# A third buffer for squares, a seventh squared group, and a new written-out order in a fused attention and rational-activation kernel

## The chip, the cores and the metric

The kernel runs on one core of one Trainium2 chip. Every time is device time in microseconds (us) of one launch. Engines are named as in the profile: PE is TensorE's matmul, PEld its weight load, DVE is VectorE, ACT is ScalarE, POOL is GpSimd, SP issues loads and stores. Of the kernel before, three runs took 264.58, 264.75 and 264.84 us; the median is 264.75.

## The reference

```python
def phi(x):                                  # q, k: [4, 4, 1088, 32]; S1, S2: [8, 32]
    a = einsum('rd,bhsd->bhsr', S1, x)
    b = einsum('rd,bhsd->bhsr', S2, x)
    return einsum('bhsi,bhsj->bhsij', a, b).reshape(..., 64)
q_p, k_p = phi(q), phi(k)
kv  = einsum('bhsf,bhsd->bhfd', k_p, v);  z = sum(k_p, axis=2)
x   = einsum('bhsf,bhfd->bhsd', q_p, kv) / (einsum('bhsf,bhf->bhs', q_p, z) + 1e-6)
x   = x with its heads side by side          # [4352, 128]
h   = x @ w_in                               # [4352, 2048]
P   = a[0] + a[1]*h + a[2]*h**2 + a[3]*h**3
Q   = 1 + abs(b[0])*abs(h) + abs(b[1])*h**2
out = (P / (Q + 1e-6)) @ w_out               # [4352, 128], float32
```

## The kernel before, in words

**Tiling.** The 4352 tokens are cut into ten chunks: two of 256 tokens (labelled 0 and 0b), seven of 512 (1 to 7), and one of 256 that holds the 64 left-over tokens of each batch (8). A chunk goes through an attention stage and then through the activation in *groups*, numbered 0 to 22: one group is some of the 16 blocks of 128 hidden columns for the tokens of one chunk. Groups 0 to 3 are chunk 0 (512, 512, 1024 and 2048 elements per partition), group 4 is chunk 0b (4096), groups 5 to 18 are two for each of the chunks 1 to 7 (4096), groups 19 to 22 are chunk 8 (2048, 1024, 512, 512).

**Attention.** Keys of a batch (`k tr`, `k ev`, `k ab`, `k eva`, `k prod`, `kv`) give kv and z in PSUM, which `kvbd`, `zbd` (DVE), `zproj` (PE), `zspread` and `zrem` (DVE) turn into weights. Queries of a chunk go through `q tr` (PE), `q ev` (ACT copy to the tile qT, line 601), `q abc` (PE), `q eva` (ACT copy to the tile abc, line 618), four small DVE steps for the denominator (`q dpr`, `q dsum`, `q dinv`, `q scale`, lines 629 to 641), `q prod` (DVE, line 646), `qp tr`, `qp ev`, `x mm` and `x ev` (ACT copy to the tile xT, line 715).

**Activation of a group g.** `h` (PE, line 794) multiplies xT by w_in into PSUM, two at a time, and `hev` (ACT, line 800) copies that to the bf16 tile hb. After that u must become |b0||h| + |b1|h*h, then 1/Q through `ln` (ACT, line 833) and `exp` (ACT, line 837: exp of minus the logarithm), and y must become the numerator. The last product y*u (`n5`, DVE, line 829) goes to PE as `py` (line 857 or 852). There are four ways, chosen by a table TERMS:

- "2" (small groups): all on DVE.
- "2d" (groups 6, 8, 10, 12, 15, 17, 19): on DVE `abs` (bitwise, line 820), `lin` (line 825), `umul` (line 829), `n1` (line 841), `n2`, `n4`, `n5` (line 829). A constant is added to y by an accumulating DMA from the tile zeros (`dadd1`, POOL, line 897). The term a0/Q is not in y; it is a second set of matmuls on u with weights scaled by a0 (`pr`, 8 matmuls of 128x512).
- "t" (groups 5, 7, 11, 13, 16, 18): on DVE `abs` (bitwise), `sq` (h*h, line 914), `sqb` (h*h times |b1|/|b0|, line 919), `n1` and `n3` (the two linear forms a3*h*h+a1 and a2*h*h+a0, line 925), `n2` (times h, line 829), `n5`. Two accumulating DMAs from tiles named lin: `dq` adds sqb's result to u, `dy` adds n3's to y. `ln` takes |b0| as a scale from the tile b_rel. No `pr`.
- "s" (groups 4, 9, 14): as "t", but the absolute value is taken by ACT (`habs`, line 809, scale |b0|) instead of DVE, `sqb` multiplies by |b1|, and `ln` has the scale 1.

At the end of a chunk `oev` (ACT, line 862), `otr` (PE, line 867) and `otev` (ACT copy to the tile oT, line 872) turn the result, and SP stores it (line 1000). Chunk 8 comes out by token and needs only one ACT copy (`otev 8`, line 982) before its store.

**Buffers.** BUFS gives the number of buffers of each tile: lin 2, xT 3, qT 2, abc 2, oT 2 and others. A tile's next use waits until an earlier user of that buffer is done; for oT this is the store's DMA, for lin that was a DMA's source it is that DMA.

**Order.** All steps are collected in a plan, and a list ORDER of step numbers, written out by hand, says in which order they are issued. Each engine runs its own instructions strictly in that order. HOT gives numbers of dummy matmuls (line 1075) that stand between the last groups on PE.

Of the kernel before, what the change touches and what calls it, by code (L numbers as in the profile page):

```python
# [12 lines left out]
FP = mybir.dt.float32  # L13
# [110 lines left out]
def kernel(  # L124
# [13 lines left out]
    nc = tc.nc  # L138
# [19 lines left out]
    TERMS = {**{g:"2d" for g in range(4,20)}, **{g:"s" for g in (4,9,14)}, **{g:"t" for g in (5,7,11,13,16,18)}}  # L158
# [3 lines left out]
    HOT = [2, 6, 23, 4, 18, 4, 3]  # L162
# [20 lines left out]
    BUFS = dict(xT=3, hb=3, u=3, lin=2, y=3, L=1, h_ps=2, out_ps=1, w_ps=2, kv_ps=1,  # L183
                kq=3, v_aug=2, kT=2, ab=2, k_p=2, qT=2, abc=2, q_p=1, q_pT=2, den=2,
                o_sb=1, oT=2)
# [129 lines left out]
    b_rel = consts.tile([128, 3], FP, name="b_rel")  # L315
# [74 lines left out]
    def rel_b():  # L390
        nc.vector.tensor_scalar(out=b_rel[:, 0:1], in0=b_abs[:, 0:1], scalar1=1e-18, scalar2=None, op0=AX.max)
        nc.vector.reciprocal(out=b_rel[:, 1:2], in_=b_rel[:, 0:1])
        nc.vector.tensor_mul(out=b_rel[:, 2:3], in0=b_rel[:, 1:2], in1=b_abs[:, 1:2])

    c_b = plan.add("DVE", 100, abs_b, after=[ld["ab"]], rank=-5)
    c_b = plan.add("DVE", 300, rel_b, after=[c_b], rank=-5) if "t" in USED else c_b
# [187 lines left out]
    def add_queries(n, nt, srcs, weights, kv_lhs, load_steps, kv_steps, w_steps, rank, give=(), early=False,  # L584
# [58 lines left out]
        def product():  # L643
            abc = T["abc", n][:, :G, :]
            T["q_p", n] = tile_of(att, "q_p", [128, JC * H, R * R], FP)
            nc.vector.tensor_mul(out=T["q_p", n][:, :G, :].rearrange("p g (i j) -> p g i j", i=R),
                                 in0=abc[:, :, 0:R, None].broadcast_to([128, G, R, R]),
                                 in1=abc[:, :, None, R:2 * R].broadcast_to([128, G, R, R]))
# [69 lines left out]
        def rest(s):  # L718
            s = plan.add("DVE", 68 + 1067 * G // 16, product, after=[s, T.get(("prod", n - 1)) if pair == 1 else None], rank=rank + 0.02, take=["q_p"],
# [59 lines left out]
    def add_group(g, G):  # L779
# [27 lines left out]
        def s_abs():  # L807
            T["u", g] = tile_of(moe, "u", [128, GW], BF)
            nc.scalar.activation(out=T["u", g][:, :gw], in_=T["hb", g][:, :gw], func=ACT.Abs, scale=b_abs[:, 0:1])  # L809
# [21 lines left out]
        def ln(l0, lw):  # L831
            T["L", g, l0] = tile_of(moe, "L", [128, LW], FP)
            nc.scalar.activation(out=T["L", g, l0][:, :lw], in_=T["u", g][:, l0:l0 + lw], func=ACT.Ln, bias=one_ap,  # L833
                                 scale=b_rel[:, 0:1] if terms == "t" else 1.0)
# [81 lines left out]
        def s_scaled():  # L916
            T["even", g] = tile_of(moe, "lin", [128, GW], BF)
            by = b_rel[:, 2:3] if terms == "t" else b_abs[:, 1:2]
            nc.vector.tensor_scalar(out=even(), in0=sq(), scalar1=by, scalar2=None, op0=AX.mult)  # L919

        def s_affine(out, c1, c0):
            def f():
                if out is y:
                    T["y", g] = tile_of(moe, "y", [128, GW], BF)
                nc.vector.tensor_scalar(out=out(), in0=sq(), scalar1=a_sb[:, c1:c1 + 1], scalar2=a_sb[:, c0:c0 + 1],  # L925
                                        op0=AX.mult, op1=AX.add)
            return f

        if square:
            sp = plan.add("DVE", tt, s_first, after=[he], rank=g - 0.5, take=["lin"], name=f"sq {g}")  # L930
            d2 = plan.add("DVE", ts + 61, s_scaled, after=[sp, c_b], rank=g - 0.5, take=["lin"], name=f"sqb {g}")
            d = add_tile("dq", u, even, [ha, d2], g - 0.5, give=["lin"])
# [17 lines left out]
        if square:  # L950
            p = plan.add("DVE", ts + 121, s_affine(y, 3, 1), after=[sp, ld["ab"]], rank=g - 0.3, take=["y"], name=f"n1 {g}")
            t = plan.add("DVE", ts + 121, s_affine(sq, 2, 0), after=[sp, d2, p, ld["ab"]], rank=g - 0.3, name=f"n3 {g}")
            p = plan.add("DVE", tt, mul(y, y, hb), after=[p, ha], rank=g - 0.3, give=["hb"], name=f"n2 {g}")
            p = add_tile("dy", y, sq, [p, t], g - 0.3, give=["lin"])
# [158 lines left out]
```

## Time and profile before

| what | value |
|---|---|
| three runs | 264.58, 264.75, 264.84 us |
| the profiled execution: its time | 264.85 us |
| the profiled execution: first to last instruction | 263.1 us |
| mean granted TensorE clock | 0.996 |
| accumulating DMAs `dq` (u<-lin), `dy` (y<-lin) | 9 and 9, 1024 KB each |
| accumulating DMAs `dadd1` (y<-zeros) | 6 of 1024 KB, 1 of 512 KB |
| dummy matmuls at line 1075 | 60, 14.2 us busy |

The profile is of one execution. Its page gives the busy time of each engine over the span of 263.1 us, a picture of the span in 40 slices, and groups of equal instructions with the mean duration of one. The trace answers further questions: who waited for whom, what ran in a given stretch, and how long one shape of instruction took. Consecutive instructions of one engine overlap a little, so starts can be closer together than durations. "Idle before" is the time that an engine stood still just ahead of an instruction, with the releaser that ended it.

### The profile page before, as it was taken

To read this page: it belongs to the slowest core of one execution; us is meant where nothing else is said; L and a number is where in the kernel's file an instruction comes from. 1 tells how busy PE (TensorE), PEld (TensorE's weight loads), DVE (VectorE), ACT (ScalarE), POOL (GpSimd) and SP (SyncE) were. 2 spreads that over 40 slices of the span, in tenths; PEclk is the share of its full clock that TensorE was granted. 3 is DMA by queue.
4 is the path that set the end of the run, shared out by engine and by line. 5 is a ranking of instruction groups with operands and counts; after the bars stand their busy time and mean duration, and the time that the engine had idled before them with its cause. 6 is when DMAs were issued, how large, how long until landed. Compare 5 with 4: busy or idle time off the path is not lost. (4 is left out here: it accounts for less than half of the span.)

```text
span 263.1 us, 3159 instructions
## 1 busy us (share of the span) xinstructions
PE 246.8 (94%) x1186; PEld 145.6 (55%) x1186; DVE 242.8 (92%) x240; ACT 238.6 (91%) x211; POOL 43.0 (16%) x63
## 2 busy tenths in 40 slices
PE   8999999999999999989899998999999899999971
PEld 4889898755656654434373645545434345554451
DVE  1658999979999999999999999999999999999992
ACT  3249798889989999999999999999999999999993
POOL 3700010101201113011201121101220202122000
PEclk9999999999999999999999999999999999999998
DMA  6969839952888996938798879972799896788812
GB/s 171 298 209 174 166 90 173 218 91 50 189 159 96 165 190 93 118 55 150 144 133 139 156 102 181 184 139 50 133 167 128 159 187 84 91 159 162 120 40 101
DMA packets 36607, 36.94 MB, mean 140 GB/s; under 512 B 18160, under 2 KB 30448, under 8 KB 36464
## 3 DMA queue, kind: packets, MB, share of 16 engines
q0 software_dynamic: 11664, 25.69, 62.6%
q1 hardware_dynamic: 24496, 10.95, 15.8%
q8 instruction: 9, 0.15, 0.2%
q10 hardware_dynamic: 432, 0.10, 0.2%
q14 instruction: 6, 0.05, 0.1%
HBM read 8.82 MB, written 2.23 MB: 42 GB/s over the span
## 5 line engine op out<-in xcount | busy, mean ns | idle before, releaser
L794 PE MATMUL h_ps<-xT,w_in_sb 128*128 128x512 f32 (+1 forms) x320 | 126.6, 533 | 0.9 <-ACT hb L800 0.9
L794 PEld LDWEIGHTS h_ps<-xT,w_in_sb 128*128 128x128 f32 x320 | 57.4, 190 | 43.4 <-issue 34.3
L800 ACT CAST hb<-h_ps 128x1024 bf16<-128x1024 f32 (+1 forms) x70 | 70.9, 1038 | 5.6 <-PE h_ps L794 5.4
L837 ACT ACTIVATE u<-L 128x4096 bf16<-128x4096 f32 (+3 forms) x23 | 63.7, 2768 | 0.3
L829 DVE TENSOR_TENSOR y<-y,hb 128x4096 bf16<-128x4096 bf16 (+3 forms) x37 | 58.7, 1595 | 0.1
L833 ACT ACTIVATE L<-u,one_ap 128x4096 f32<-128x4096 bf16 (+3 forms) x17 | 43.4, 2555 | 0.2 <-DVE u L829 0.2
L829 DVE TENSOR_TENSOR y<-y,u 128x4096 bf16<-128x4096 bf16 (+3 forms) x23 | 39.8, 1731 | 0.5 <-ACT u L837 0.3
L857 PEld LDWEIGHTS <-w_out 128*128 128x128 bf16 x208 | 20.2, 98 | 27.6 <-issue 11.8
L857 PE MATMUL out_ps<-y,w_out 128*128 128x512 bf16 (+1 forms) x144 | 30.8, 355 | 1.1 <-DVE y L829 1.1
L897 POOL DMA_DIRECT2D u<-lin x9 | 10.8, 1206 | 104.4 <-ACT ab L461 25.7
L833 ACT ACTIVATE L<-u,one_ap,b_rel 128x4096 f32<-128x4096 bf16 x6 | 23.2, 3875 | 0.0
L914 DVE TENSOR_TENSOR lin<-hb 128x4096 bf16<-128x4096 bf16 x9 | 20.6, 2287 | 0.0
L897 POOL DMA_DIRECT2D y<-lin x9 | 12.0, 1334 | 49.6 <-DVE y L829 15.7
L829 DVE TENSOR_TENSOR u<-lin,u 128x4096 bf16<-128x4096 bf16 (+3 forms) x14 | 19.2, 1375 | 0.2
L897 POOL DMA_DIRECT2D y<-zeros x7 | 12.3, 1760 | 41.6 <-PE h_ps L794 18.4
L820 DVE TENSOR_SCALAR u<-hb 128x4096 int16<-128x4096 int16 (+3 forms) x20 | 18.4, 918 | 0.5 <-ACT hb L800 0.3
L489 PEld LDWEIGHTS kv_ps<-v_aug,k_p 128*128 128x128 f32 x128 | 15.3, 192 | 1.1 <-issue 0.2
L489 PE MATMUL kv_ps<-v_aug,k_p 128*128 128x66 f32 x128 | 15.8, 272 | 0.0
L857 PE MATMUL out_ps<-u,w_out 128*128 128x512 bf16 (+1 forms) x64 | 13.7, 352 | 1.3 <-ACT u L837 1.1
L1075 PE MATMUL kv_ps<-const-float32-0.0 128*128 128x512 bf16 x60 | 14.2, 381 | 0.0
L661 ACT COPY q_pT<-w_ps 128x512 f32<-128x512 f32 (+1 forms) x20 | 10.5, 552 | 2.6 <-PE w_ps L654 2.6
L841 DVE TENSOR_SCALAR y<-hb,a_sb 128x4096 bf16<-128x4096 bf16 (+3 forms) x14 | 12.4, 886 | 0.0
(102 smaller groups left out, 274.1 us busy)
## 6 DMA issues: line engine op xcount, KB each, us to landing
u<-lin POOLq DMA_DIRECT2D x9, 1024.0 KB, 7.9
y<-lin POOLq DMA_DIRECT2D x9, 1024.0 KB, 8.2
y<-zeros POOLq DMA_DIRECT2D x6, 1024.0 KB, 11.0
out_dram<-oT SPq DMA_DIRECT2D x7, 256.0 KB, 2.7
kq<-in_k_dram SPq DMA_DIRECT2D x3, 512.0 KB, 5.0
v_aug<-in_v_dram SPq DMA_DIRECT2D x12, 128.0 KB, 4.7
kq<-in_q_dram SPq DMA_DIRECT2D x3, 512.0 KB, 4.8
w_in_sb<-in_moe_w_in_dram SPq DMA_DIRECT2D x1, 1024.0 KB, 6.9
```

The source lines that it names most:

```text
L489: nc.tensor.matmul(T["kv", b][:, hp * 66:(hp + 1) * 66], lhsT=lhs(hp), rhs=rhs(hp), start=(first and hp == 0), stop=final, skip_group_chec ...
L794: nc.tensor.matmul(T["h", g, s][:, i * W:(i + 1) * W], lhsT=w_in_sb[:, fi * 128:(fi + 1) * 128], rhs=T["xT", n][:, :W], start=True, stop=True)
L800: nc.scalar.copy(out=T["hb", g][:, s * W:(s + nsub) * W], in_=T["h", g, s][:, :nsub * W])
L820: nc.vector.tensor_scalar(out=u().bitcast(mybir.dt.int16), in0=hb().bitcast(mybir.dt.int16), scalar1=0x7FFF, scalar2=None, op0=AX.bitwise_and)
L829: return lambda: nc.vector.tensor_mul(out=out(), in0=in0(), in1=in1())
L833: nc.scalar.activation(out=T["L", g, l0][:, :lw], in_=T["u", g][:, l0:l0 + lw], func=ACT.Ln, bias=one_ap, scale=b_rel[:, 0:1] if terms == ...
L837: nc.scalar.activation(out=T["u", g][:, l0:l0 + lw], in_=T["L", g, l0][:, :lw], func=ACT.Exp, scale=-1.0)
L841: nc.vector.tensor_scalar(out=y(), in0=hb(), scalar1=a_sb[:, 3:4], scalar2=a_sb[:, 2:3], op0=AX.mult, op1=AX.add)
L857: nc.tensor.matmul(T["o", n][:, :W], lhsT=W_terms[w][:, fis[i], :], rhs=T[src, g][:, i * W:(i + 1) * W], start=(start and i == 0), stop=(s ...
L897: nc.gpsimd.dma_start(out=dst(), in_=src(), accum_op=AX.add, max_dma_last_dim=4096)
L914: nc.vector.tensor_mul(out=sq(), in0=hb(), in1=hb())
L1075: nc.tensor.matmul(hot_ps[0], lhsT=zero.broadcast_to([128, 128]), rhs=zero.broadcast_to([128, CW]), start=True, stop=True)
```

## The change

1. BUFS: lin 2 to 3; xT 3 to 2; qT, abc and oT 2 to 1.
2. "s" groups: the factor |b1| moves from `sqb` into the scales. `habs` multiplies by |b0|/|b1|, `ln` by |b1|, and `sqb` is dropped; `dq` adds the plain square. `n3` therefore writes a new lin tile and no longer overwrites the square, and `dq` is issued after `n3`.
3. Group 8 goes from "2d" to "t".
4. One small instruction more in `rel_b` (the tile b_rel now holds both ratios).
5. A new ORDER and a new HOT (63 dummy matmuls in 8 places, not 60 in 7).

`q prod` can also be put on POOL by a set QPOOL, but that set is empty.

```diff
-    TERMS = {**{g:"2d" for g in range(4,20)}, **{g:"s" for g in (4,9,14)}, **{g:"t" for g in (5,7,11,13,16,18)}}
+    TERMS = {**{g:"2d" for g in range(4,20)}, **{g:"s" for g in (4,9,14)}, **{g:"t" for g in (5,7,11,13,16,18,8)}}
-    HOT = [2, 6, 23, 4, 18, 4, 3]
+    QPOOL = set()
+    HOT = [7, 1, 24, 9, 5, 7, 6, 4]
...
-    BUFS = dict(xT=3, hb=3, u=3, lin=2, y=3, L=1, h_ps=2, out_ps=1, w_ps=2, kv_ps=1,
-                kq=3, v_aug=2, kT=2, ab=2, k_p=2, qT=2, abc=2, q_p=1, q_pT=2, den=2,
-                o_sb=1, oT=2)
+    BUFS = dict(xT=2, hb=3, u=3, lin=3, y=3, L=1, h_ps=2, out_ps=1, w_ps=2, kv_ps=1,
+                kq=3, v_aug=2, kT=2, ab=2, k_p=2, qT=1, abc=1, q_p=1, q_pT=2, den=2,
+                o_sb=1, oT=1)
...
-        nc.vector.tensor_scalar(out=b_rel[:, 0:1], in0=b_abs[:, 0:1], scalar1=1e-18, scalar2=None, op0=AX.max)
-        nc.vector.reciprocal(out=b_rel[:, 1:2], in_=b_rel[:, 0:1])
-        nc.vector.tensor_mul(out=b_rel[:, 2:3], in0=b_rel[:, 1:2], in1=b_abs[:, 1:2])
+        nc.vector.tensor_scalar(out=b_rel[:, 0:2], in0=b_abs[:, 0:2], scalar1=1e-18, scalar2=None, op0=AX.max)
+        nc.vector.reciprocal(out=b_rel[:, 2:4], in_=b_rel[:, 0:2])
+        nc.vector.tensor_mul(out=b_rel[:, 4:5], in0=b_rel[:, 2:3], in1=b_abs[:, 1:2])
+        nc.vector.tensor_mul(out=b_rel[:, 5:6], in0=b_rel[:, 3:4], in1=b_abs[:, 0:1])
...
-            nc.scalar.activation(out=T["u", g][:, :gw], in_=T["hb", g][:, :gw], func=ACT.Abs, scale=b_abs[:, 0:1])
+            nc.scalar.activation(out=T["u", g][:, :gw], in_=T["hb", g][:, :gw], func=ACT.Abs, scale=b_rel[:, 5:6])
...
-                                 scale=b_rel[:, 0:1] if terms == "t" else 1.0)
+                                 scale={"t": b_rel[:, 0:1], "s": b_rel[:, 1:2]}.get(terms, 1.0))
...
-            d2 = plan.add("DVE", ts + 61, s_scaled, after=[sp, c_b], rank=g - 0.5, take=["lin"], name=f"sqb {g}")
-            d = add_tile("dq", u, even, [ha, d2], g - 0.5, give=["lin"])
+            if wide_abs:
+                d1 = plan.add("DVE", ts + 121, s_affine(y, 3, 1), after=[sp, ld["ab"]], rank=g - 0.45, take=["y"], name=f"n1 {g}")
+                t = plan.add("DVE", ts + 121, s_affine(even, 2, 0), after=[sp, d1, ld["ab"]], rank=g - 0.45, take=["lin"], name=f"n3 {g}")
+                d = add_tile("dq", u, sq, [ha, t], g - 0.5, give=["lin"])
+            else:
+                d2 = plan.add("DVE", ts + 61, s_scaled, after=[sp, c_b], rank=g - 0.5, take=["lin"], name=f"sqb {g}")
+                d = add_tile("dq", u, even, [ha, d2], g - 0.5, give=["lin"])
```

What the new order does around the places that the prediction speaks of, read from the two lists engine by engine:

- DVE: group 8's `sq`, `sqb`, `abs` stand behind `n5 5` and `n4 6`; behind group 9's `sq` come `n1`, `n3`. The steps from `n5 18` to the end are the same set in nearly the same order.
- ACT: the same 212 steps. `otev 3` moves up to between `ln 19` and `exp 19`, `otev 6` to between `ln 20` and `exp 20`, `otev 7` to just ahead of `ln 22`; `otev 8` stays last.
- PE: `pr 8` is gone. `q tr 2` to `q tr 4` and with them the loads that wait for their buffers move later, `q tr 6` moves far up.
- POOL: `dq 8`, `dy 8` in the place of `dadd1 8`.

More of the change, by code (lines that the diff above doesn't have):

```diff
@@ L314 @@
     b_abs = consts.tile([128, 2], FP, name="b_abs")
-    b_rel = consts.tile([128, 3], FP, name="b_rel")
+    b_rel = consts.tile([128, 6], FP, name="b_rel")
     c_add = {i: zeros if i == ADDED[0] else big.tile([128, CW], FP, name=f"c_add{i}") for i in ADDED}
@@ L390, in rel_b @@
     def rel_b():
-        nc.vector.tensor_scalar(out=b_rel[:, 0:1], in0=b_abs[:, 0:1], scalar1=1e-18, scalar2=None, op0=AX.max)
-        nc.vector.reciprocal(out=b_rel[:, 1:2], in_=b_rel[:, 0:1])
-        nc.vector.tensor_mul(out=b_rel[:, 2:3], in0=b_rel[:, 1:2], in1=b_abs[:, 1:2])
+        nc.vector.tensor_scalar(out=b_rel[:, 0:2], in0=b_abs[:, 0:2], scalar1=1e-18, scalar2=None, op0=AX.max)
+        nc.vector.reciprocal(out=b_rel[:, 2:4], in_=b_rel[:, 0:2])
+        nc.vector.tensor_mul(out=b_rel[:, 4:5], in0=b_rel[:, 2:3], in1=b_abs[:, 1:2])
+        nc.vector.tensor_mul(out=b_rel[:, 5:6], in0=b_rel[:, 3:4], in1=b_abs[:, 0:1])
     c_b = plan.add("DVE", 100, abs_b, after=[ld["ab"]], rank=-5)
-    c_b = plan.add("DVE", 300, rel_b, after=[c_b], rank=-5) if "t" in USED else c_b
+    c_b = plan.add("DVE", 400, rel_b, after=[c_b], rank=-5) if USED & {"s", "t"} else c_b
     def scaled(i, col, half):
@@ L645, in product @@
             T["q_p", n] = tile_of(att, "q_p", [128, JC * H, R * R], FP)
-            nc.vector.tensor_mul(out=T["q_p", n][:, :G, :].rearrange("p g (i j) -> p g i j", i=R),
-                                 in0=abc[:, :, 0:R, None].broadcast_to([128, G, R, R]),
-                                 in1=abc[:, :, None, R:2 * R].broadcast_to([128, G, R, R]))
+            eng = nc.gpsimd if n in QPOOL else nc.vector
+            eng.tensor_mul(out=T["q_p", n][:, :G, :].rearrange("p g (i j) -> p g i j", i=R),
+                           in0=abc[:, :, 0:R, None].broadcast_to([128, G, R, R]),
+                           in1=abc[:, :, None, R:2 * R].broadcast_to([128, G, R, R]))
         def p_transposes(hp):
@@ L718, in rest @@
         def rest(s):
-            s = plan.add("DVE", 68 + 1067 * G // 16, product, after=[s, T.get(("prod", n - 1)) if pair == 1 else None], rank=rank + 0.02, take=["q_p"],
+            s = plan.add("POOL" if n in QPOOL else "DVE", 2300 * G // 16 if n in QPOOL else 68 + 1067 * G // 16, product, after=[s, T.get(("prod", n - 1)) if pair == 1 else None], rank=rank + 0.02, take=["q_p"],
                          give=[] if pair == 0 else ["abc"] + ([] if early else ["den"]), name=f"q prod {lab(n)}")
@@ L917, in s_scaled @@
             T["even", g] = tile_of(moe, "lin", [128, GW], BF)
-            by = b_rel[:, 2:3] if terms == "t" else b_abs[:, 1:2]
-            nc.vector.tensor_scalar(out=even(), in0=sq(), scalar1=by, scalar2=None, op0=AX.mult)
+            nc.vector.tensor_scalar(out=even(), in0=sq(), scalar1=b_rel[:, 4:5], scalar2=None, op0=AX.mult)
         def s_affine(out, c1, c0):
             def f():
-                if out is y:
-                    T["y", g] = tile_of(moe, "y", [128, GW], BF)
+                if out is not sq:
+                    name = "y" if out is y else "lin"
+                    T["y" if out is y else "even", g] = tile_of(moe, name, [128, GW], BF)
                 nc.vector.tensor_scalar(out=out(), in0=sq(), scalar1=a_sb[:, c1:c1 + 1], scalar2=a_sb[:, c0:c0 + 1],
@@ L950, in add_group @@
         if square:
[L951 to L954, printed above, removed]
+            if not wide_abs:
+                d1 = plan.add("DVE", ts + 121, s_affine(y, 3, 1), after=[sp, ld["ab"]], rank=g - 0.3, take=["y"], name=f"n1 {g}")
+                t = plan.add("DVE", ts + 121, s_affine(sq, 2, 0), after=[sp, d2, d1, ld["ab"]], rank=g - 0.3, name=f"n3 {g}")
+            p = plan.add("DVE", tt, mul(y, y, hb), after=[d1, ha], rank=g - 0.3, give=["hb"], name=f"n2 {g}")
+            p = add_tile("dy", y, even if wide_abs else sq, [p, t], g - 0.3, give=["lin"])
         else:
```

70 rows, old and new, of the table ORDER are left out of this document.

## The prediction

> **What bounds the kernel now.** I read the page's busy shares first, then the stretches, then the last wait on DVE, then single durations. Three engines are above 90%, so the shares alone name no bound:
>
> ```profile
> PE 246.8 (94%) x1186; PEld 145.6 (55%) x1186; DVE 242.8 (92%) x240; ACT 238.6 (91%) x211; POOL 43.0 (16%) x63
> ...
> PEclk9999999999999999999999999999999999999998
> ```
>
> The stretches separate them (columns: stretch, its length, then busy time and count of PE, PEld, DVE, ACT, POOL; clock; DMA share; GB/s). I cut at 54.30, where DVE last waits for long, and at 246.20, where `n5 18` starts:
>
> ```profile
> 17.00:102.00 85.00, 85.00 (x460) 59.70 (x461) 81.66 (x103) 77.80 (x82) 11.12 (x8) 1.00 0.80 147
> 54.30:246.20 191.90, 185.05 (x772) 96.68 (x770) 190.74 (x142) 189.25 (x141) 32.66 (x23) 1.00 0.82 132
> 246.20:263.10 16.90, 9.36 (x89) 5.90 (x87) 11.66 (x22) 12.17 (x16) 0.00 (x0) 0.94 0.34 87
> ```
>
> From 17 to 102 us PE has no gap at all. From 54.3 to 246.2 DVE is busy 190.74 of 191.90 us: its list of work sets the end of that stretch. ACT is close behind with 2.65 us to spare. The seam between both is visible at the end of the stretch, and so is the wait that opened it:
>
> ```profile
> 54.30 0.43 DVE L629 TENSOR_TENSOR den<-abc 128x256 f32<-128x256 f32 x1 [1.19 <-ACT abc L618]
> ...
> 245.19 0.69 DVE L829 TENSOR_TENSOR u<-lin,u 128x1024 bf16<-128x1024 bf16 x1
> 246.16 2.29 DVE L829 TENSOR_TENSOR y<-y,u 128x4096 bf16<-128x4096 bf16 x1 [0.28 <-ACT u L837]
> ```
>
> `n5 18` (246.16) waits 0.28 us for `exp 18` on ACT: after 192 us both arrive within 0.3 us of each other. So time comes off only if **both** get there sooner: DVE by less work, ACT by fewer waits. After `n5 18` comes a tail of 16.9 us in which the last groups are finished.
>
> **The change, part by part.** Durations (count, busy us, mean ns):
>
> ```profile
> L914 DVE TENSOR_TENSOR lin<-hb 128x4096 bf16<-128x4096 bf16 x9 | 20.6, 2287 | 0.0
> L829 DVE TENSOR_TENSOR u<-lin,u 128x4096 bf16<-128x4096 bf16 x6 | 13.7, 2288 | 0.0
> L825 DVE TENSOR_SCALAR lin<-u,b_abs 128x4096 bf16<-128x4096 bf16 x6 | 8.0, 1327 | 0.0
> L919 DVE TENSOR_SCALAR lin<-lin,b_rel 128x4096 bf16<-128x4096 bf16 x6 | 7.7, 1281 | 0.0
> L925 DVE TENSOR_SCALAR lin<-lin,a_sb 128x4096 bf16<-128x4096 bf16 x9 | 12.2, 1360 | 0.0
> L919 DVE TENSOR_SCALAR lin<-lin,b_abs 128x4096 bf16<-128x4096 bf16 x3 | 3.9, 1285 | 0.1
> L833 ACT ACTIVATE L<-u,one_ap 128x4096 f32<-128x4096 bf16 x9 | 34.1, 3793 | 0.0
> L833 ACT ACTIVATE L<-u,one_ap,b_rel 128x4096 f32<-128x4096 bf16 x6 | 23.2, 3875 | 0.0
> ```
>
> *DVE.* Each "s" group loses one `sqb` of 1.285 us; neighbours overlap by about 0.09 (two products at 90.08 take 4.49, not 4.57), so 1.2 each. Group 4's lies ahead of the 1.19 us wait at 54.30, which ends on ACT and PE, so it only lengthens that wait: 0. Groups 9 and 14: 2.4. Group 8 loses `lin`, `umul`, `n4` (1.33 + 2.29 + 2.29 = 5.91) and gains `sq`, `sqb`, `n3` (2.29 + 1.28 + 1.36 = 4.93): 1.0. In the stretch DVE has **3.4 us** less to do. The extra `rel_b` instruction (its kin near 23 us take 0.16) lies ahead of the same wait: 0.
>
> *ACT.* Four logarithms (groups 4, 8, 9, 14) get a scale from memory: 3875 - 3793 = 82 ns each, 0.33 us. Its spare 2.65 becomes 2.3. That is no sharp limit: an ACT instruction that follows another starts about 0.1 us before that one ends (`exp 18` at 242.51 takes 3.62, the next starts at 246.03), an overlap that every wait forfeits and the busy time does not show. So ACT can give 2.3 us by its idle time, and more with overlaps; DVE can give 3.4.
>
> *PE.* `pr 8` goes: eight matmuls, 1.73 us start to start (126.93 to 128.66). PE has 6.85 us spare in the long stretch, but none before 102 us, so I looked at whether the new order feeds ACT later. For each ACT step that waits for PE I added the PE work ahead of it and the ACT work behind it up to `exp 18`, start-to-start spacings from the trace. The largest sum was 221.4 us (`x ev 3`) in the old list and is 220.1 (`hev 7,2`) in the new: 1.3 us better, not worse. Three more dummy matmuls at 0.21 us stand in PE's late idle time: 0.
>
> *Buffers.* lin: DVE's list of waits has no wait for a DMA but the first load, so the third buffer removes none by itself; it lets groups 7, 8, 9 square one after another. In the new list `sqb 8` needs `dq 7` landed; about 10 us of DVE work lie between. `n3 9` needs `dq 8`: 13 us. Landings are in the next fence, so 0, 10 us each if none of that work stood between. xT: `x ev` now needs the last `h` of two chunks back, which stands far ahead in PE's list: 0. qT: `q ev 7` needs `q abc 6`, which the next ACT step needs anyway: 0 to 0.48. abc: `q eva 8` needs `q prod 7`, four DVE steps ahead of the step that reads it: 0.
>
> *SP and POOL.* `q tr 3` moves from 39 to about 49 us, and SP's load of k for batch 3, which waits for its buffer, with it; by its 8.9 us landing it is there at 58, its reader `k tr (3, 0)` comes near 66. POOL trades one DMA for two:
>
> ```profile
> u<-lin POOLq DMA_DIRECT2D x9, 1024.0 KB, 7.9
> y<-lin POOLq DMA_DIRECT2D x9, 1024.0 KB, 8.2
> y<-zeros POOLq DMA_DIRECT2D x6, 1024.0 KB, 11.0
> ...
> out_dram<-oT SPq DMA_DIRECT2D x7, 256.0 KB, 2.7
> ```
>
> That is 5.1 us more of transfer near 95 to 115 us, behind 17 us of ACT work ahead of `ln 8`: 0.
>
> *Tail.* From `exp 18` on both lists hold the same work, but `otev 7` now stands ahead of `ln 22`. Before, `ln 22` waited 0.21 us for DVE; with 0.47 more ACT work ahead it starts 0.2 later. And with one oT buffer each `otev` waits for the store before. The four stores here landed in 2.0 us (median), all stores in 2.7. By spacing, `otev 7` would end at 256.7, its store lands at 258.8 or 259.5, and `otev 8` is due at 258.95: 0 to 0.5. Behind `otev 8` is only the final store. I take **+0.3**, of 0.2 to 0.7.
>
> *Sum.* The end of the long stretch moves by 2.3 (ACT's idle time) to 3.4 us (DVE's work), if the engines mesh as now. As each then waits for the other more often, I take 2.6, near the ACT row. 264.85 - 2.6 + 0.3 = 262.55 for the profiled execution; the median of the runs is 0.1 lower: **262.5**.
>
> **Rivals.**
> - *DVE was the only bound.* Everything follows its list: -3.4 + 0.2 gives 261.6. For it: DVE's 190.74 of 191.90. Against it: ACT's 2.3. 0.12.
> - *ACT is the bound and does not compress.* `n5 18` already waits for ACT; then 0.33 us of logarithms and 0.3 of tail are added and a part of PE's 1.3 comes off: 264.75 + 0.6 - 0.5, about 264.9. Against it: ACT's 2.65 us of waits came while DVE held what PE needed next. 0.12.
> - *Crowded DMAs.* With groups 7, 8, 9 in a row, `ln 7` may wait for `dq 7`, which landed 9.4 us after 85.58, 4 us ahead of `ln 7` (98.97). `sqb 7` now stands one 1.3 us step later. Beyond a landing of 12 us each us costs one, on ACT: at 14.5, 264.9. 0.05.
> - *Slower: the single output buffer.* If stores land late in the tail, `otev 3`, `6`, `7` hold up ACT and the logarithms behind them. The price is one us per us above 2.2; at 4.5 us the gain is gone. The slowest store in the trace took 6.1: 262.5 + 4.0 = 266.5. Against it: the last four took 2.0. 0.10.
> - *A slower TensorE clock.* The clock row is at 9 until the last slice (0.94 in the tail's row), and PE's longest waits are near 1 us; a shorter PE list could make longer ones. One slice of 6.6 us at half the clock ahead of 102 us, where PE has no gap, would cost up to 3.3 us; behind it PE's 6.85 us of spare time hides most. 262.5 to 265.8, 0.03. [...]
>
> **How the numbers follow.** Forecast 0.58 (261.8 to 264.0), rivals as above. About 0.2% (0.53 us) is what a measurement of this kernel can tell from no change. Faster: 0.58 + 0.12 + 0.03 and a part of the crowded case, 0.77; within 0.2%: the ACT case and the rest of the crowded case, 0.13; slower: 0.10. The range goes from 261.2 (DVE's 3.4 with no loss in the tail) to 264.9 (ACT and crowded cases); the store case is left out.
>
> **What would show it.** Right: 238 DVE instructions (240 - 3 + 1), none that scales by b_abs from lin to lin; `n5 18` near 243.5 with a longer wait for `exp 18`; ACT's idle time from 54 us to there down to about 1 us; eight matmuls of u fewer. Wrong: `n5 18` still at 246 (ACT rival); a wait of `otev` for a store (slower rival); `ln` waiting for a DMA (crowded); DVE waiting for more than 1.5 us in all for evacuations, which would mean that the new order meshes worse than the old.

## The result, and the profile after

The changed kernel takes **265.89 us** (median of 16 runs, 264.36 to 268.52) against 264.82 us (16 runs, 264.5 to 265.1) for the kernel before: a ratio of 1.0048, interval 1.0029 to 1.0068 (ratios are formed from the single runs, not from the two medians). It is slower, by about 1.1 us; the prediction said 2.3 us faster. In 5 of its 16 runs the mean granted clock was 0.980 or lower, and those are the five longest (267.3 to 268.5 us); the other eleven have a median of 265.54 us, still 0.7 us above the kernel before. The profiled execution took 265.92 us, with a span of 264.2 us and a clock of 0.995.

The busy line of the page, and the two stretches that the prediction is built on:

```profile
PE 245.3 (93%) x1170; PEld 145.1 (55%) x1181; DVE 239.4 (91%) x238; ACT 238.1 (90%) x211; POOL 42.7 (16%) x64
...
PEclk9999999999999999999999999999999999999997
```

```profile
54.30:246.20 191.90, 183.61 (x762) 96.64 (x770) 188.68 (x140) 190.40 (x145) 32.26 (x24) 1.00 0.84 138
246.20:264.20 18.00, 9.29 (x87) 5.61 (x84) 11.26 (x22) 10.86 (x14) 0.00 (x0) 0.93 0.22 71
```

DVE is down to 238 instructions and 2.1 us less busy in the long stretch, as intended. But ACT is now busy for 190.40 of 191.90 us. These are all of DVE's waits above 0.15 us in that stretch, and `n5 18`, which ends it (start, duration, in brackets the wait just ahead and what ended it):

```profile
54.79 0.43 DVE L631 TENSOR_TENSOR den<-abc 128x256 f32<-128x256 f32 x1 [1.29 <-ACT abc L620]
95.70 2.29 DVE L917 TENSOR_TENSOR lin<-hb 128x4096 bf16<-128x4096 bf16 x1 [0.19 <-ACT hb L803]
133.80 2.29 DVE L917 TENSOR_TENSOR lin<-hb 128x4096 bf16<-128x4096 bf16 x1 [0.47 <-ACT hb L803]
187.45 1.49 DVE L844 TENSOR_SCALAR y<-hb,a_sb 128x4096 bf16<-128x4096 bf16 x1 [0.68 <-ACT hb L803]
...
245.59 2.29 DVE L832 TENSOR_TENSOR y<-y,u 128x4096 bf16<-128x4096 bf16 x1
```

`n5 18` starts 0.57 us earlier than before (245.59 against 246.16), not 2.6. From the wait near 54 us to `n5 18` DVE has 2.6 us less busy time (188.68 without 0.61 of `n5 18`, against 190.74 without 0.04) but 1.6 us more idle time, and it started there 0.5 us later. Of the 1.6 us, 0.9 are in the waits shown (the kernel before has 0.17 and 0.28 us there); the rest is in gaps of about 0.1 us and less. `exp 18` on ACT ends 1.1 us earlier, so here DVE is the later one.

From `n5 18` to the end of the span the kernel before took 16.9 us and the changed one 18.6. ACT's list in that stretch shows where the 1.7 us went. The kernel before (`ln 19`, then `exp 19`):

```profile
246.98 2.02 ACT L833 ACTIVATE L<-u,one_ap 128x2048 f32<-128x2048 bf16 x1
249.03 1.91 ACT L837 ACTIVATE u<-L 128x2048 bf16<-128x2048 f32 x1
```

The changed kernel:

```profile
245.87 2.02 ACT L836 ACTIVATE L<-u,one_ap 128x2048 f32<-128x2048 bf16 x1
250.06 0.58 ACT L875 COPY oT<-w_ps 128x512 f32<-128x512 f32 x1 [2.17 <-DMA out_dram<-oT]
250.54 1.91 ACT L840 ACTIVATE u<-L 128x2048 bf16<-128x2048 f32 x1
```

The copy is `otev 3`. With one oT buffer it waits 2.17 us for the store of `otev 5`, and `exp 19` stands behind it: it starts 4.95 us after `n5 18`, against 2.87 before. That store in the kernel before, the same store in the changed kernel, and the next one there (issue, size, time to landing in us):

```profile
out_dram<-oT SPq DMA_DIRECT2D x1, 256.0 KB, 2.9
```

```profile
out_dram<-oT SPq DMA_DIRECT2D x1, 256.0 KB, 4.5
```

```profile
out_dram<-oT SPq DMA_DIRECT2D x1, 256.0 KB, 2.0
```

So there were two things to test. **Theory:** the tail loses its time to this wait, and the rest of the change is a small gain. **Rival:** the new order costs the time, and the wait lies beside other work. And apart from both: why did a cut of DVE's work that was put at 3.4 us bring 0.6?

### The profile page after: what moved, and what is told of

It is laid out like the page before. It is cut to its first block, busy times and chain, and to the rows that moved or that the text cites. A ratio compares the mean times of both kernels' runs of the same rounds, so it can differ in the third digit from the quotient of the medians.

```text
span 264.2 us, 3143 instructions
## 1 busy us (share of the span) xinstructions
PE 245.3 (93%) x1170; PEld 145.1 (55%) x1181; DVE 239.4 (91%) x238; ACT 238.1 (90%) x211; POOL 42.7 (16%) x64
## 4 chain that ended last, share of the span: by engine, by line
ACT 31%; PE 26%; DVE 24%; issue 11%; DMA 6%; ACTq 0%; DVEq 0%
PE h_ps L797 12%; DVE y L832 9%; ACT hb L803 9%; ACT L L836 8%; ACT u L840 6%; PE kv_ps L491 4%; DMA y<-lin 4%; DVE lin L917 3%; ACT u L812 2%; DVE u L823 2%; DVE lin L921 2%; PE w_ps L455 2%; DVE u L832 2%; DMA out_dram<-oT 2%; PE out_ps L354 1%
## 5 line engine op out<-in xcount | busy, mean ns | idle before, releaser
L803 ACT CAST hb<-h_ps 128x1024 bf16<-128x1024 f32 (+1 forms) x70 | 72.6, 1053 | 3.6 <-PE h_ps L797 3.5
L832 DVE TENSOR_TENSOR y<-y,hb 128x4096 bf16<-128x4096 bf16 (+3 forms) x36 | 56.4, 1574 | 0.3
L836 ACT ACTIVATE L<-u,one_ap,b_rel 128x4096 f32<-128x4096 bf16 x10 | 38.9, 3894 | 0.0
L900 POOL DMA_DIRECT2D u<-lin x10 | 12.4, 1243 | 104.4 <-ACT ab L463 28.2
L836 ACT ACTIVATE L<-u,one_ap 128x4096 f32<-128x4096 bf16 (+3 forms) x13 | 28.2, 2173 | 0.0
L917 DVE TENSOR_TENSOR lin<-hb 128x4096 bf16<-128x4096 bf16 x10 | 22.8, 2284 | 1.2 <-ACT hb L803 1.2
L832 DVE TENSOR_TENSOR u<-lin,u 128x4096 bf16<-128x4096 bf16 (+3 forms) x13 | 16.9, 1301 | 0.2
L900 POOL DMA_DIRECT2D y<-zeros x6 | 9.1, 1518 | 34.9 <-DVE y L832 13.2
L928 DVE TENSOR_SCALAR y<-lin,a_sb 128x4096 bf16<-128x4096 bf16 x10 | 13.4, 1342 | 0.3
L928 DVE TENSOR_SCALAR lin<-lin,a_sb 128x4096 bf16<-128x4096 bf16 x10 | 13.5, 1347 | 0.0
```

The costliest lines, as they stand in the source:

```text
L803: nc.scalar.copy(out=T["hb", g][:, s * W:(s + nsub) * W], in_=T["h", g, s][:, :nsub * W])
L832: return lambda: nc.vector.tensor_mul(out=out(), in0=in0(), in1=in1())
L900: nc.gpsimd.dma_start(out=dst(), in_=src(), accum_op=AX.add, max_dma_last_dim=4096)
L917: nc.vector.tensor_mul(out=sq(), in0=hb(), in1=hb())
```

## Experiments on the tail

**Two oT buffers in the changed kernel** (`one_ap` moves into a spare column of b_rel).

```diff
-    one_ap = consts.tile([128, 1], FP, name="one_ap")
-    b_rel = consts.tile([128, 6], FP, name="b_rel")
+    b_rel = consts.tile([128, 7], FP, name="b_rel")
+    one_ap = b_rel[:, 6:7]
...
-                o_sb=1, oT=1)
+                o_sb=1, oT=2)
```

> The changed kernel with one edit: two output buffers oT instead of one (the constant one moves into a column of b_rel to make room), order and all else as changed. Theory A (the tail loses about 2.1 us because otev 3 waits 2.2 us for the store of otev 5, which took 4.5 us; the stretch before it gained 1.1 us): no wait of otev for a store, tail as long as before the change, 263.7 to 264.0 us, and its runs lie as close together as those of the kernel before. Rival B (the order in the tail and the meshing of DVE and ACT cost the time; ACT's wait for the store lies beside work of DVE that must be done anyway): no wait for a store either, but 265.4 to 265.9 us.

Measured: 264.51 us (12 runs, 264.02 to 266.75), ratio 1.0007, interval 0.9984 to 1.0031. The wait for the store is gone and the tail is back at 17.0 us (`n5 18` at 245.73, span 262.7), although that store took 4.9 us here. One number in BUFS brings 1.4 us of median, or 1.6 when each is set against the kernel before as measured with it (264.82 and 265.03 us). The theory holds for the tail; the median lies above its 263.7 to 264.0. Not as expected: the runs do not close up. Seven lie at 264.0 to 264.6 (clock 0.991 or more), five at 266.2 to 266.8 (0.982 to 0.984).

**The old places of the copies on ACT, still one buffer** (the list by step names; `otev 7` moves from ahead of `ln 22` to behind `exp 22`).

```diff
 ACT: ln 19
-otev 3
 exp 19, oev 7, ln 20
-otev 6
-exp 20
+exp 20, otev 6
 ...
+exp 21, otev 3
 ...
+exp 22, otev 7
```

> The changed kernel with a single oT buffer, but otev 6, 3 and 7 stand on ACT where they stood before the change (behind exp 20, exp 21 and exp 22). Theory A: otev 3 comes some 4 us later, after the store of otev 5 has landed, so the wait goes although the buffer stays single; but otev 6, 3, 7 and 8 then follow each other more closely, so some of the wait can come back: 263.9 to 264.5 us. Rival B: 265.4 to 265.9 us.

Measured: 266.50 us (7 runs, 266.07 to 269.0), ratio 1.0066, interval 1.0038 to 1.0094. Both forecasts were too low. `otev 3` now waits 0.25 us, but the wait has moved to the end: `otev 7` waits 0.59 and `otev 8` 2.11 us for the store ahead of it. Neither of the two orders hides it; four copies and their stores of 2.0 us and more have to pass one buffer one by one.

**The kernel before with one oT buffer.** Each store is now issued right behind its copy; nothing else differs:

> The kernel before with a single oT buffer, nothing else (each store stands right behind its evacuation in the order). If the single buffer costs what the changed kernel with two of them suggests: its tail holds three evacuations of 128x512 within 5 us, against stores of 2.0 us and more: 266.0 to 267.0 us. If the single buffer only costs in the changed order: 264.9 to 265.3 us.

Measured: 267.48 us (4 runs), ratio 1.0099, interval 1.0086 to 1.0112: 2.6 us, more than expected. ACT's waits from 240 us on are the same two kinds (us in total, times, longest):

```profile
ACT oT L982 <- DMA out_dram<-oT: 2.1, 1, 2.1
ACT oT L872 <- DMA out_dram<-oT: 1.0, 2, 0.8
```

This settles that the single buffer costs time by itself, in the old order even more than in the new one.

**Why the store took 4.5 us.** In the changed kernel with one buffer, the last accumulating DMA is left out:

```diff
+                if name != "dadd1" or g != 19:
                     nc.gpsimd.dma_start(out=dst(), in_=src(), accum_op=AX.add, ...)
```

> The changed kernel with its single oT buffer; the last accumulating DMA of all (the constant 1 added to y of group 19, 512 KB, issued near 240 us) is left out. Theory (the store of otev 5 takes 4.5 us because its packets stand behind that DMA's; the last stores, with none beside them, take 2.0): that store lands in 2.0 to 2.8 us, otev 3 waits at most 0.5 us instead of 2.2, 264.2 to 264.7 us. Rival (the store is late for a reason of its own): it takes 4 us or more again, 265.5 to 266.0 us.

Measured: 265.27 us (12 runs, 263.87 to 268.25; 4 of them at a clock near 0.98). The store took 3.4 us and `otev 3` waited 1.11, between the two forecasts. What the accumulating DMA costs the store is not shown by this: with that DMA the same store took 4.1, 4.5 and 4.9 us in three traces of the new order (`a_tail`, the changed kernel, two oT buffers), but 2.9 us in two of the old order (the kernel before, with two oT buffers and with one), and 3.4, from a single trace, lies between the two. Nor is it a matter of busy DMA engines alone: in the trace of the changed kernel they are busy for a share of 0.04 and 0.03 from 248 to 250 us, while the store has not landed. Why it is late stays open.

## Experiments on the long stretch

**The buffers of before in the new order** (lin 2, xT 3, qT 2, abc 2, oT 2).

> The changed kernel with its new order and terms, but all buffer numbers of before (lin 2, xT 3, qT 2, abc 2, oT 2). Theory A: the wait for the store is gone; the third lin buffer is what lets groups 7, 8 and 9 square in a row, so with two of them squares wait for landings: two waits of up to 4 us on DVE in the stretch from 80 to 120 us, part of it covered: 264 to 268 us. If the third lin buffer does nothing: as with two oT buffers alone, 263.7 to 264.0 us. Rival B: no better than 265.4 us in either case.

Measured: 272.97 us (5 runs), ratio 1.0308, interval 1.0287 to 1.0328. The direction was expected, the size was not: 8.5 us above the same order with three lin buffers. DVE waits for landings in three places, 8.6 us together:

```profile
101.06 1.29 DVE L921 TENSOR_SCALAR lin<-lin,b_rel 128x4096 bf16<-128x4096 bf16 x1 [2.86 <-DMA y<-lin]
121.04 1.34 DVE L928 TENSOR_SCALAR lin<-lin,a_sb 128x4096 bf16<-128x4096 bf16 x1 [4.30 <-DMA y<-lin]
...
187.09 1.35 DVE L928 TENSOR_SCALAR lin<-lin,a_sb 128x4096 bf16<-128x4096 bf16 x1 [1.40 <-DMA y<-lin]
```

So without the third lin buffer the new order loses time. The change gives four other tiles one buffer less along with it, and oT is the one that hurt.

**Only the fold of b, in the kernel before.** Steps `sqb` 4, 9 and 14 go, order and buffers stay:

```diff
-            d2 = plan.add("DVE", ts + 61, s_scaled, ...)
-            d = add_tile("dq", u, even, [ha, d2], ...)
+            d = add_tile("dq", u, sq, [ha, t], ...)
...
-                                 scale=b_rel[:, 0:1] if terms == "t" else 1.0)
+                                 scale={"t": b_rel[:, 0:1], "s": b_rel[:, 1:2]}.get(terms, 1.0))
```

> The kernel before with one part of the change: b folded into the scales of the three s groups (sqb 4, 9 and 14 left off DVE, three logarithms with a scale from memory on ACT); its order, its buffers and its six t groups stay. If DVE alone were the bound of the long stretch: two times 1.2 us less, 262.4 us. Theory A (both bind; what DVE sheds it waits away for ACT, which gains 0.25 us of work): 0.3 to 1.0 us less, 263.8 to 264.5 us. If ACT alone were the bound: no gain, 264.8 to 265.1 us.

Measured: 264.95 us (11 runs) against 265.03, ratio 0.9996, interval 0.9987 to 1.0005. Of 2.4 us less on DVE nothing arrives that is clear of noise. DVE's waits in the stretch show where it is handed back:

```profile
122.87 1.35 DVE L844 TENSOR_SCALAR y<-hb,a_sb 128x4096 bf16<-128x4096 bf16 x1 [0.31 <-PE out_ps L860]
133.83 2.29 DVE L917 TENSOR_TENSOR lin<-hb 128x4096 bf16<-128x4096 bf16 x1 [0.61 <-ACT hb L803]
188.14 1.34 DVE L844 TENSOR_SCALAR y<-hb,a_sb 128x4096 bf16<-128x4096 bf16 x1 [1.25 <-ACT hb L803]
246.26 2.29 DVE L832 TENSOR_TENSOR y<-y,u 128x4096 bf16<-128x4096 bf16 x1 [0.27 <-ACT u L840]
```

The 1.2 us of `sqb 9` (near 113 us) come back as 0.31 and 0.61 us, those of `sqb 14` (near 179) as the 1.25 us ahead of `n1 15`, which needs `hev 15,6` (the last of the four copies that fill hb of group 15). The chain of waits of the same run hardly touches DVE:

```profile
PE 42%; ACT 41%; DVE 9%; issue 7%; ACTq 0%; DVEq 0%
```

**Is it ACT, then?** The exponential of group 12 left out, in the kernel before and with the fold:

```diff
+            if g != 12:
                 nc.scalar.activation(out=T["u", g]..., func=ACT.Exp, scale=-1.0)
```

> The kernel before, with the exponential of group 12 left out (its u stays the square; 3.6 us less on ACT, nothing else changed). If ACT alone bound the long stretch: 3.3 us less, 261.7 us. If DVE and ACT both bind: DVE's list is as long as it was and waits for ACT only 0.3 us at its end and 1.2 us at its start, so 0.2 to 0.8 us less, 264.2 to 264.8 us.

> The kernel before with b folded into the scales of the three s groups (2.4 us less on DVE in the long stretch, which by itself brought nothing) and, again, the exponential of group 12 left out. If both engines bind: now DVE's 2.4 us show as well, 262.0 to 262.8 us, some 2 us below the kernel before without that exponential. If ACT alone bound: 261.5 to 261.9 us, the same as the kernel before without that exponential. If neither (TensorE's order): both stay above 264.5 us.

Measured: 264.91 us (11 runs; ratio 1.0002, 0.9993 to 1.0010) and 264.72 us (12 runs; 0.9998, 0.9988 to 1.0007). ACT alone is not the bound, but with both engines relieved the time does not move either: of the cases for the second kernel this is the last, in which neither engine's list alone sets the time. The 3.6 us reappear as one wait of ACT, 3.7 us for PE (`qp tr 6`), and PE waits there for `q prod 6` of DVE. It was the wrong exponential to leave out: nobody later needed ACT sooner.

**The logarithm of group 13 left out**, right ahead of `hev 15,6`:

```diff
+            if g == 13:
+                return
             T["L", g, l0] = tile_of(moe, "L", [128, LW], FP)
...
+            src = T["u", g][:, l0:l0 + lw] if g == 13 else T["L", g, l0][:, :lw]
```

> The kernel before with b folded into the scales (2.4 us less on DVE), and the logarithm of group 13 left out (its exponential reads u instead of L): 3.6 us less on ACT between 182 and 186 us, right ahead of hev 15,6, for which n1 15 on DVE waits 1.25 us in the fold alone. Theory (DVE's saving lies wholly ahead of n1 15, and n1 15 cannot start before ACT has done hev 15,6, so the saving is waited away there): that wait goes and so does the 0.27 us ahead of n5 18, 1.3 to 1.6 us less than before, 263.2 to 263.6 us. Rival (no cut of DVE or ACT counts, as without the exponential of group 12): 264.5 us or more. Rival (ACT alone binds): 261.5 us.

> The kernel before, with the logarithm of group 13 left out in the same way. Theory: DVE reaches n1 15 no sooner, since it has its full list, and no wait to lose there: 0 to 0.3 us less, 264.5 to 264.9 us; the difference from the kernel with the fold is then what the fold is worth once ACT does not stand in the way, 1.0 to 1.4 us. Rival (ACT alone binds): 261.5 us.

Measured: 264.12 us with the fold (11 runs; 0.9978, 0.9967 to 0.9989) and 264.42 without (11 runs; 0.9988, 0.9973 to 1.0003). The kernel without the fold came out 0.1 us below its range, the one with it gained half of what was expected: the fold is worth 0.3 us here, at the edge of the noise, not 1.0 to 1.4. DVE's wait went from 1.25 to 0.65 us only, and ACT now waits for PE at `hev 15,4`:

```profile
187.22 1.53 DVE L847 TENSOR_SCALAR y<-hb,a_sb 128x4096 bf16<-128x4096 bf16 x1 [0.65 <-ACT hb L803]
```

```profile
185.26 1.93 ACT L803 CAST hb<-h_ps 128x1024 bf16<-128x1024 f32 x2 [3.00 <-PE h_ps L797]
```

**And `pr 12` (eight matmuls on PE ahead of `h 15`) left out as well:**

```diff
-                              lambda l0=l0, lw=lw: project("u", 0, ...),
+                              (lambda: None) if g == 12 else lambda l0=l0, lw=lw: project("u", 0, ...),
```

> The kernel before with b folded into the scales, without the logarithm of group 13 (ACT, 3.6 us ahead of hev 15,6) and now also without pr 12 (eight matmuls, 1.73 us on TensorE, ahead of h 15,6). Theory (the three engines stand abreast at n1 15: with the logarithm gone DVE still waited 0.65 us, for hev 15,6, which waited 3.0 us for TensorE): the wait ahead of n1 15 goes altogether, 0.6 us less than without the logarithm alone: 263.3 to 263.7 us. Rival (TensorE is not what holds hev 15,6): 264.0 to 264.3 us, as without the logarithm alone.

> The kernel before without the logarithm of group 13 and without pr 12; the fold is not in it. Theory: DVE has its full list up to n1 15 and now holds the others up alone, so no gain over leaving out the logarithm: 264.2 to 264.6 us; against the same kernel with the fold, the fold is then worth 0.7 to 1.2 us, where by itself it brought 0.1. Rival (a cut of TensorE's list counts by itself): 263.6 us or less, and no difference from the kernel with the fold.

Measured: 264.34 us with the fold (11 runs; 0.9983, 0.9975 to 0.9992) and 264.43 without (11 runs; 0.9986, 0.9977 to 0.9995). The theory of three lists abreast falls: with 1.73 us less on PE the wait ahead of `n1 15` is still there. PE only came to wait itself, for the copy to xT:

```profile
187.27 1.35 DVE L847 TENSOR_SCALAR y<-hb,a_sb 128x4096 bf16<-128x4096 bf16 x1 [0.53 <-ACT hb L803]
```

```profile
172.95 1.07 PE L657 MATMUL w_ps<-ident,q_p 128*128 128x128 f32 x8 [0.19 <-DVE den L631]
174.26 1.56 PE L670 MATMUL w_ps<-q_pT,kv_bd 128*64 128x512 f32 x4 [0.24 <-ACT q_pT L664]
177.07 3.70 PE L797 MATMUL h_ps<-xT,w_in_sb 128*128 128x512 f32 x8 [1.25 <-ACT xT L718]
```

Read from below: `h 15` waits for `x ev 6`, that for `x mm 6`, that for `qp ev 6`, that for `qp tr 6`, and that for `q prod 6` on DVE (the first row names den, a step of 0.22 us right behind `q prod 6`; what `qp tr 6` reads is q_p, which `q prod 6` writes). It is not a list but a chain of dependences, which leaves DVE at `q prod 6` and comes back to it at `n1 15` some 15 us later. `sqb 14` lies between the two, beside the chain. The chain of waits of the kernel before begins with the same steps and then, from `x ev 6` on (176.22), follows ACT's list (start, us, what):

```profile
171.41 1.23 DVE q_p L646
...
172.79 0.64 PE w_ps L654 x4
...
173.45 1.07 ACT q_pT L661 x2
174.52 1.19 ACT hb L800 x2
...
176.22 0.63 ACT xT L715
176.85 3.60 ACT u L809
180.45 1.82 ACT hb L800 x2
182.26 3.02 ACT L L833
...
185.81 1.98 ACT hb L800 x2
...
187.81 1.35 DVE y L841
```

There DVE arrives at `n1 15` just as `hev 15,6` is done, so the trace shows no wait. Counted from the start of `q prod 6`, `n1 15` starts 16.40 us later in the kernel before and 16.42 with the fold, 15.80 without the logarithm as well, and 15.69 without `pr 12` too. So besides DVE's own list two more paths end there: ACT's list, as long as DVE's, and the chain through PE, some 0.7 us shorter; either holds `n1 15`. That both would have to be shortened together with the fold is read from the traces; no run here did it.

**Work left out behind `n1 15`,** the product `n2 16` on DVE and the exponential of group 16 on ACT:

```diff
+            if g != 16:
                 nc.scalar.activation(out=T["u", g]..., func=ACT.Exp, scale=-1.0)
...
-            p = plan.add("DVE", tt, mul(y, y, hb), after=[p, ha], ..., name=f"n2 {g}")
+            p = plan.add("DVE", tt, (lambda: None) if g == 16 else mul(y, y, hb), after=[p, ha], ..., name=f"n2 {g}")
```

> The kernel before, with work left out behind n1 15 (187.8 us): the product n2 16 (2.2 us on DVE, near 206 us) and the exponential of group 16 (3.6 us on ACT, near 225 us). Theory (from n1 15 to n5 18 DVE runs without a gap, ACT with 0.3 us to spare, so that here both cuts count at once): 2.0 to 2.3 us less, 262.5 to 262.9 us, where the fold and the exponential of group 12 together, 2.4 us of DVE and 3.6 us of ACT ahead of n1 15, brought 0.1. Rival (another thing, PE's order or a DMA, sets the end): 264.5 us or more.

Measured: 263.38 us (6 runs), ratio 0.9958, interval 0.9944 to 0.9972. That is 1.45 us, two thirds of the forecast, and by far the most that any cut brought. What is missing is seen at `n5 14`: DVE, without the product, is free for it at 206.1 and waits there 1.01 us for `exp 14`, since ACT was relieved only later:

```profile
207.14 2.29 DVE L829 TENSOR_TENSOR y<-y,u 128x4096 bf16<-128x4096 bf16 x1 [1.01 <-ACT u L838]
```

Of 2.2 us 1.2 remain, and the 0.28 us ahead of `n5 18` are gone too.

## Experiments on the clock, and a faster version

**Dummy matmuls in PE's idle time.** The run of the old ACT order above (`a_tail`) was profiled in an execution with a mean clock of 0.978, and it is the only traced execution with so low a clock. Its stretches of 2 us (after POOL: clock, DMA share, GB/s):

```profile
166.00:168.00 2.00, 1.30 (x9) 0.91 (x8) 1.97 (x2) 2.00 (x1) 0.07 (x1) 1.00 0.73 131
168.00:170.00 2.00, 0.66 (x4) 0.42 (x4) 2.00 (x2) 2.00 (x5) 0.00 (x0) 1.00 1.09 197
170.00:172.00 2.00, 1.84 (x4) 0.29 (x4) 2.00 (x3) 1.51 (x3) 0.70 (x1) 0.54 1.08 197
172.00:174.00 2.00, 1.31 (x4) 0.67 (x3) 2.00 (x1) 1.82 (x2) 0.48 (x1) 0.50 0.54 98
174.00:176.00 2.00, 2.00 (x4) 0.51 (x2) 2.00 (x2) 2.00 (x1) 0.00 (x0) 0.50 1.09 197
176.00:178.00 2.00, 1.95 (x12) 0.97 (x13) 0.30 (x1) 0.92 (x3) 0.00 (x0) 0.75 1.06 193
```

PE is busy for 1.30 and 0.66 of 2 us, then the clock is at half until about 177 us; DVE then has 0.30 and ACT 0.92 of 2 us. The new order has this idle place on PE, where it waits three times for short copies on ACT (1.45, 0.74 and 0.81 us in the changed kernel). The waits alone do not decide: in the traces of the changed kernel and of the one with two oT buffers they are the same within 0.15 us, and the clock stays at 1.00. Twelve dummy matmuls (6, 3, 3) go there, in the changed kernel with two oT buffers (the order is shown by step names):

```diff
-    HOT = [7, 1, 24, 9, 5, 7, 6, 4]
+    HOT = [6, 3, 3, 7, 1, 24, 9, 5, 7, 6, 4]
 PE: otr 2
+hot 0
 qp tr 6,1
+hot 1
 x mm 6
+hot 2
```

> The changed kernel with two oT buffers, and 12 dummy matmuls (6, 3 and 3) put into the three waits of TensorE between 166.9 and 172 us (1.45, 0.74 and 0.81 us), which stand only 0.6 and 1 us apart. Theory (the runs of the changed kernel that come out 2 us longer have the granted clock at half from about 170 to 177 us, because TensorE is idle for 3 of 5 us there): the clock stays above 0.99 in every run, all runs between 264.0 and 264.7 us, median 264.3 us. Rival (what varies sits in the tail or elsewhere): as with two oT buffers alone, some 4 in 10 runs still near 266.4 us.

Measured: 264.38 us (12 runs, 264.10 to 266.15), ratio 0.9987, interval 0.9975 to 0.9999. No clock below 0.991; eleven runs lie within 264.1 to 264.7, one, at 266.15, does not fit. Of the four kernels above with the new order and three lin buffers, 16 of 47 runs had a clock of 0.984 or less; here it was none of 12, and none of 11 in the next version. Two things limit this. The versions with these dummies ran on another chip than the three of those four kernels whose chip is on record, and no run without them was made on it. And the old order is not free of low clocks: one of the 11 runs of the kernel with only the fold took 272.25 us at a clock of 0.964.

**Group 17 as a "t" group too**, in that version: `lin 17`, `umul 17`, `n4 17`, `pr 17` and `dadd1 17` go, `sq 17`, `sqb 17`, `n3 17`, `dq 17` and `dy 17` come.

```diff
-    TERMS = {..., **{g:"t" for g in (5,7,11,13,16,18,8)}}
+    TERMS = {..., **{g:"t" for g in (5,7,11,13,16,18,8,17)}}
```

> The changed kernel with two oT buffers and the dummy matmuls, and group 17 made into a t group as well, as the change did with group 8: 1.0 us less on DVE and 1.7 us less on TensorE, but behind n1 15, where DVE runs without a wait up to n5 18 and comes 0.5 us behind ACT. Theory (a cut of DVE counts where DVE has no wait behind it): 0.4 to 0.6 us less than with group 17 as it was, 263.8 to 264.0 us. Rival (two more 1 MB accumulating DMAs between 210 and 230 us bring waits for landings): 264.5 to 267 us.

Measured: 264.22 us (11 runs, 263.99 to 264.56), ratio 0.9981, interval 0.9973 to 0.9990. It beats both kernels, the one before by 0.6 us. `n5 18` starts 0.8 us earlier than without it (245.01 against 245.83) and now waits for ACT. But 0.3 of the 0.8 us are already there near 54 us (54.66 against 54.96), ahead of all that differs. So of the 1.0 us less on DVE 0.5 counted, which is what DVE came behind ACT before, and 0.4 are waited for `exp 18`. The tail gives back 0.3, one wait for a landing appears in it, and the medians differ by 0.16 only, short of the forecast and not clear of noise:

```profile
245.01 2.29 DVE L832 TENSOR_TENSOR y<-y,u 128x4096 bf16<-128x4096 bf16 x1 [0.43 <-ACT u L840]
249.68 1.23 DVE L832 TENSOR_TENSOR y<-y,hb 128x2048 bf16<-128x2048 bf16 x1 [0.21 <-DMA y<-zeros]
```

## Why the prediction was wrong, point by point

- **The long stretch, -2.6: wrong, 0.57 came.** DVE's list did get shorter (2.6 us of busy time, not 3.4) and ACT's idle time did shrink (2.65 to 1.50 us). The step that failed is the reading of DVE's busy time, "its list of work sets the end of that stretch". A sum over 192 us assumes that time saved at 113 or 179 us is still there at 246. All of DVE's cuts lie ahead of `n1 15`, where another path of equal length arrives, and in the old order the fold alone is worth 0.1 us, not clear of noise. The prediction cited one meeting of two engines, `n5 18` at 246.16, and did not look for the others; the chain of waits of the kernel before showed the one at 187.81. In the changed kernel the meeting at `n1 15` takes back 0.68 us; two smaller waits, small gaps and the later start near 54 us take back the rest, and what causes the gaps and the later start stays open.
- **Tail +0.3: mis-sized, 1.7 measured.** The mechanism was named, both as a step and as the slower rival, with its price of one us per us above 2.2. The landing was read from the median of the four last stores, 2.0 us, which is below that price. The store that mattered was the one of `otev 5`, which took 2.9 us before and 4.5 after. The row of that store would have given 0.7 us; the other 1.6 no row of the kernel before could give. The rival had a chance of 0.10 and a time of 266.5, and 265.9 came, but that it comes so near is luck: it took a store of 6.1 us and the full gain ahead of the tail; with 4.5 us its price gives 264.8.
- **The sum** for the profiled executions, with what was measured: 264.85 - 0.57 + 1.67 = 265.95, against 265.92.
- **The slower clock: there, and underrated at 0.03.** "PE's longest waits are near 1 us" was true of the old order. The new order puts waits of 1.45, 0.74 and 0.81 us close together, and 5 of the 16 runs of the changed kernel lost 2.6 us (median 268.12 us, against 265.54 for the others). Whether the waits are the cause is made likely by the dummies, with the limits named there.
- **Third lin buffer at 0: right only as a statement on the kernel before.** In the new order it is worth 8.5 us, and the single oT buffer that came with it was the loss.
- **Right:** 238 DVE instructions, eight matmuls fewer (1186 weight loads became 1181, with three dummies more), no wait of `ln` for a DMA, no cost from xT, qT and abc that any wait shows.
- **Open:** why the fold, the third buffer and the order together gain 0.5 us (the version with two oT buffers and dummies against the kernel before) was not split further between group 8 and the order.

## What to carry to other kernels

A saving on a nearly full engine is worth what is left of it at the next place where that engine waits for, or just meets, another path; so follow the chain of waits from the cut forward to the end, and do not sum busy time over a long stretch. When a buffer count goes to one, look up the duration of the very transfer that the next user waits for, not a median. After any reordering, add up an engine's short waits that stand close together, on TensorE above all: here they were 1.45, 0.74 and 0.81 us in the new order, and 16 of 47 of its runs without the dummies there had a clock of 0.984 or less.

## What the runs showed of the hardware

- **In one trace the granted clock fell after two short gaps close together.** In the traced execution of `a_tail` PE was idle for 1.46 and 0.74 us up to 170.2 us, with 0.66 us of matmuls between; then the clock stayed at half (0.50 in the stretches from 172 to 176 us) until about 177 us. In the trace of the changed kernel waits of 1.45 and 0.74 us at the same place passed at a clock of 1.00. What decides between the two is not shown.
- **Stores of 256 KB from SBUF took 2.0 to 4.9 us in the tail.** With an accumulating DMA in flight the store of `otev 5` took 2.9 us in two traces of the old order and 4.1, 4.5 and 4.9 us in three of the new; without it 3.4 us, in one trace. The three stores of 256 KB behind it took 2.0 us each in the kernel before and in the changed one.
